# A fused convolution and feed-forward kernel: order and size of the first weight loads, and three matmul units ahead of the first sums of half group 1

## Chip, cores, metric

One core of one Trainium2 chip. The metric is the device time of one execution in microseconds; the "span" of a profile is the time from the first to the last instruction, and lies some 1.7 us below the time of the same execution. Lower is better. Before: 693.21 us (median of 3 runs, 693.14 to 693.33).

## The reference, cut to what matters

```python
w = softmax(weight)                        # 8 heads x 7 taps
x_pad = zeros of 6 rows ahead of x         # x: 8 x 4096 x 192
conv[b, s, h, g] = sum_k w[h, k] * x_pad[b, s + k, h, g]
h = conv.reshape(32768, 192) @ w_in        # 192 x 2048
out = maximum(0.01 * h, h) @ w_out         # 2048 x 192
```

## The kernel before

Everything is kept transposed: channels in the partitions, two batch rows side by side (64 + 64 partitions), three chunks of 64 channels. The first blocks of 512 positions are worked in half groups of 256, so that work can start before much has been loaded. A *unit* of the first matmul makes two of the sixteen 128-wide slices of the hidden layer for one half group: 12 matmuls into one `ph` buffer, which ScalarE evicts through the leaky ReLU into `g`. There are two `ph` buffers. The *sums* are the second matmul, in steps of 32 matmuls.

```python
    pieces = (0, NFC // 4, NFC // 2, NFC)             # NFC = 16; w_in in three tiles: 1/4, 1/4, 1/2
    ...
    def w_in_of(f, ps, c):
        n = max(n for n in range(3) if pieces[n] <= f)
        a = (f // RUN * RUN - pieces[n]) * 128 + f % RUN
        return w_in[n][ps, c, a : a - f % RUN + RUN * 128 : RUN]

    load_w_in(0, 0)                                   # all of these on GpSimd's queue, in this order
    ident = const_pool.tile([128, 128], BF16)
    make_identity(nc, ident)
    load_w_in(0, 1)
    for e in range(2):
        load_w_in(1, e)
    load_first(1)                                     # half 1's x (x_rows)
    for e in range(2):
        load_w_in(2, e)
    load_first(2)                                     # half 2's x
    ...                                               # then w_out, half 3's x, block 2
```

```python
    warm(9)                                           # dummy matmuls, 128x256
    warm(1, 128)
    ...
    select(wps_hm, slice(0, 2))                       # six small matmuls: the taps by channel
    warm(1, 128)
    select(wps_l, 2)                                  # six more
    warm(6)
    ...
    transpose_first(0)                                # half 0's x, on TensorE
    warm(3)
    ...                                               # half group 0's convolution, partly on TensorE (56 matmuls)

        for j in range(steps):
            for u in range(2 * j, 2 * j + 2):
                mm1(grp, u)                           # one unit
                if i == 0 and u == 1:
                    transpose_first(1)                # needs half 1's x
                    evac_first(1, nc.vector.tensor_copy, nc.vector.tensor_copy)
                    ...                               # half group 1's convolution: a chunk on TensorE, two on VectorE
                if i == 0 and u == 3:
                    for job in pe_ahead:
                        job()                         # 28 matmuls
                    evac_y(act_scale)
                if i == 0 and u == 6:
                    transpose_first(2)
            ...
            for _ in range(quota[j]):                 # 0 in half group 0, then 16: one step of sums
                mm2_slot(slot)
                slot += 1
```

Of the kernel before, what the change touches and what calls it, by code (L numbers as in the profile page):

```python
# [14 lines left out]
def kernel(  # L15
# [25 lines left out]
    NFC = F // 128  # L41
# [73 lines left out]
    def load_first(q):  # L115
        rows = x[0:2, q * HT : (q + 1) * HT, :].rearrange("e (s p) d -> p e s d", s=HS)
        if q == 0:
            x_nat[q] = stage_pool.tile([128, 2, HS, D], FP32, name="x_nat")
            for e in range(2):
                nc.sync.dma_start(out=x_nat[q][:, e], in_=rows[:, e])  # L120
        elif q in x_rows:
            for e in range(2):
                nc.gpsimd.dma_start(out=x_rows[q][:, e], in_=rows[:, e])  # L123
        else:
            for c in range(NCH):
                for e in range(2):
                    nc.gpsimd.dma_start(  # L127
                        out=x_half[q][:, c, :, e, :],
                        in_=rows[:, e, :, c * CH : (c + 1) * CH],
                    )  # L130
# [9 lines left out]
    def transpose_first(q):  # L140
        ts = [
            psum_o.tile([128, HS, NCH, CH], BF16, name=f"ptr{i}", tag="po") for i in range(2)
        ]
        for s in range(HS):
            for c in range(NCH):
                for i in range(2):
                    ps = slice(i * CH, (i + 1) * CH)
                    if q in x_half:
                        nc.tensor.transpose(  # L149
                            out=ts[i][:, s, c, :],  # L150
                            in_=x_half[q][ps, c, s, :, :].rearrange("p e k -> p (e k)"),
                            identity=ident[ps, ps],
                        )
                        continue
                    for e in range(2):
                        nc.tensor.transpose(  # L156
                            out=ts[i][e * CH : (e + 1) * CH, s, c, :],
                            in_=x_rows[q][ps, e, s, c * CH : (c + 1) * CH],
                            identity=ident[ps, ps],
                        )  # L160
        ptr[q] = ts

    def evac_first(q, *copies):
        dst = xt[0][:, :, HALO + q * HT : HALO + (q + 1) * HT].rearrange(
            "p c (s i k) -> p i s c k", s=HS, i=2
        )
        for i, t in enumerate(ptr.pop(q)):
            copies[i](out=dst[:, i], in_=t)  # L168
# [4 lines left out]
    def conv_jobs(grp, chunks=range(NCH)):  # L173
        blk, t0, T = grp
        rp, st = divmod(blk, NB)
        if blk not in yt:
            yt[blk] = yt_pool.tile([128, NCH, ST], BF16, name="yt")
        y = yt[blk]
        jobs = []
        for c in chunks:  # L180
            for k in range(K):
                a = BASE + k + st * ST + t0
                src = xt[rp][:, c, a : a + T]
                dst = y[:, c, t0 : t0 + T]
                if k == 0:
                    jobs.append(
                        lambda s=src, d=dst, c=c: nc.vector.tensor_scalar_mul(  # L187
                            d, s, wk[:, c, 0:1]
                        )
                    )  # L190
                else:
                    jobs.append(
                        lambda s=src, d=dst, c=c, k=k: nc.vector.scalar_tensor_tensor(  # L193
                            out=d, in0=s, scalar=wk[:, c, k : k + 1], in1=d,
                            op0=mybir.AluOpType.mult, op1=mybir.AluOpType.add,
                        )
                    )
        return jobs
# [39 lines left out]
        )  # L238


    pieces = (0, NFC // 4, NFC // 2, NFC)
    w_in = [
        const_pool.tile([128, NCH, (b - a) * 128], BF16, name=f"w_in{a}")
        for a, b in zip(pieces[:-1], pieces[1:])
# [2 lines left out]
    def load_w_in(n, e):  # L247
        fs = slice(pieces[n] * 128, pieces[n + 1] * 128)
        nc.gpsimd.dma_start(  # L249
            out=w_in[n][e * CH : (e + 1) * CH],  # L250
            in_=moe_w_in[:, fs].rearrange("(c p) f -> p c f", p=CH),
        )

    def w_in_of(f, ps, c):
        n = max(n for n in range(3) if pieces[n] <= f)
        a = (f // RUN * RUN - pieces[n]) * 128 + f % RUN
        return w_in[n][ps, c, a : a - f % RUN + RUN * 128 : RUN]

# [1 line left out]
    ident = const_pool.tile([128, 128], BF16)  # L260
    make_identity(nc, ident)
    load_w_in(0, 1)
    for e in range(2):
        load_w_in(1, e)
    load_first(1)
    for e in range(2):
        load_w_in(2, e)
    load_first(2)


# [122 lines left out]
    def mm1(grp, u):  # L393
        blk, t0, T = grp
        y = yt[blk]
        nf = ST // T
        ph = psum_h.tile([128, 2, ST], FP32, name="ph", tag="ph")
        for i in range(nf):
            f = nf * u + i
            for c in range(NCH):  # L400
                for e in range(2):
                    ps = slice(e * CH, (e + 1) * CH)
                    nc.tensor.matmul(  # L403
                        out=ph[:, e, i * T : (i + 1) * T],
                        lhsT=w_in_of(f, ps, c),
                        rhs=y[ps, c, t0 : t0 + T],
                        start=(c == 0),
                        stop=(c == NCH - 1),
                    )
        act = nc.scalar.activation(  # L410
            out=g[blk][:, nf * u : nf * (u + 1), :, t0 : t0 + T],
            in_=ph.rearrange("p e (i t) -> p i e t", i=nf),
            func=mybir.ActivationFunctionType.Prelu, alpha=0.01,
        )
        return act
# [83 lines left out]
    for i, grp in enumerate(groups):  # L499
        blk, t0, T = grp  # L500
        steps = T // 64
        if t0 == 0:
            g[blk] = g_pool.tile([128, NFC, 2, ST], BF16, name="g", tag="g")
        quota = plan.get(i, [(avail - slot) // steps] * steps)

        if i == 0:
            ahead = []
        else:
            ahead = conv_jobs(groups[i + 1]) if i + 1 < len(groups) else []
        per = -(-len(ahead) // steps)  # L510
        for j in range(steps):
            for u in range(2 * j, 2 * j + 2):
                mm1(grp, u)
                if i == 0 and u == 1:
                    transpose_first(1)
                    evac_first(1, nc.vector.tensor_copy, nc.vector.tensor_copy)
                    pe_ahead, evac_y = pe_conv_jobs(groups[1], 0)
                    ahead = conv_jobs(groups[1], range(1, NCH))
                    per = len(ahead)
                if i == 0 and u == 3:  # L520

                    for job in pe_ahead:
                        job()
# [3 lines that stand above are left out]
            if i == 1 and j == 3:  # L527
                transpose_first(3)
            jobs = ahead[per * j : per * (j + 1)]
            if T == ST:  # L530


                jobs = ahead[len(ahead) * j // steps : len(ahead) * (j + 1) // steps]
                for job in jobs:
                    job()
                jobs = []
            for _ in range(quota[j]):
                mm2_slot(slot)
                slot += 1
            if i == 0 and j == 3:  # L540
                evac_first(2, nc.vector.tensor_copy, nc.vector.tensor_copy)
            if i == 2 and j == 1:
                transpose_x(2)
            for job in jobs:
                job()
            if i == 1 and j == 3:
                evac_first(3, nc.vector.tensor_copy, nc.vector.tensor_copy)

            last_half = t0 + T == ST
            if j == steps // 4 and last_half:  # L550
                load_x(blk + 3)
            if j == steps // 2 and last_half and blk > 0:
                transpose_x(blk + 2)
        avail += 2 * T // 128 * NFC
# [36 lines left out]
```

## Time and profile before

| what (us from the start) | before |
|---|---|
| time, span of the profiled run | 693.21; 690.9 |
| TensorE busy | 684.0 of 690.9 |
| second part of the first unit starts | 10.15 |
| first sums start | 22.48 |
| between the two | 12.33 |
| w_in's first tile, second tile landed | 8.1, 11.8 |
| half 1's x landed | 13.0 |
| third w_in tile, half 2's x, w_out landed | 16.8, 17.8, 21.6 |

Landings are read from the trace's landing records, and a landing here is the last of a transfer's 16 records: for the two parts of half 1's x these came at 12.50 and 13.03, and TensorE's waits for them ended at 12.55 and 13.07.

The timeline of TensorE stands in the prediction. Columns: start, length, engine, line, operation, operands, shapes, count, and in brackets the idle time before it and what ended it.

```profile
6.33 3.26 PE L212 MATMUL acc<-xt,diag 64*64 64x256 bf16 x56 [0.17 <-ACT xt L168]
```

The 56 matmuls take 3.26 us, 58 ns each: TensorE at full clock, by the clock record of this trace (1.0 from 5.38 us on).

### The profile page before, as it was taken

To read this page: it belongs to the slowest core of one execution; us is meant where nothing else is said; L and a number is where in the kernel's file an instruction comes from. 1 tells how busy PE (TensorE), PEld (TensorE's weight loads), DVE (VectorE), ACT (ScalarE), POOL (GpSimd) and SP (SyncE) were. 2 spreads that over 40 slices of the span, in tenths; PEclk is the share of its full clock that TensorE was granted. 3 is DMA by queue.
4 is the path that set the end of the run, shared out by engine and by line. 5 is a ranking of instruction groups with operands and counts; after the bars stand their busy time and mean duration, and the time that the engine had idled before them with its cause. 6 is when DMAs were issued, how large, how long until landed. Compare 5 with 4: busy or idle time off the path is not lost.

```text
span 690.9 us, 26980 instructions
## 1 busy us (share of the span) xinstructions
PE 684.0 (99%) x12188; PEld 599.2 (87%) x12188; DVE 550.1 (80%) x1051; ACT 527.0 (76%) x609; POOL 147.1 (21%) x206
## 2 busy tenths in 40 slices
PE   8999999999999999999999999999999999999998
PEld 6999999999988888888888888888888888888887
DVE  6999999999986787878787878877878878787812
ACT  6888888888898777777777777777777777777771
POOL 7822220222222202222102222102222112000000
PEclk9999999999999999999999999999999999999999
DMA  9976454556649445566445565445664455322112
GB/s 153 117 92 94 76 79 82 68 75 83 82 71 94 72 81 74 67 93 82 67 84 68 75 83 87 74 74 76 77 82 74 81 73 70 67 60 59 47 42 65
DMA packets 184163, 53.85 MB, mean 78 GB/s; under 512 B 149104, under 2 KB 183664, under 8 KB 184048
## 3 DMA queue, kind: packets, MB, share of 16 engines
q0 software_dynamic: 99536, 14.76, 30.2%
q1 hardware_dynamic: 84512, 37.38, 22.8%
q8 instruction: 95, 1.56, 1.0%
q14 instruction: 20, 0.16, 0.1%
HBM read 29.88 MB, written 25.17 MB: 80 GB/s over the span
## 4 chain that ended last, share of the span: by engine, by line
PE 96%; ACT 1%; DMA 1%; POOL 1%; issue 0%; DVE 0%; POOLq 0%
PE po L429 49%; PE ph L403 47%; ACT g L410 1%; DMA w_in<-in_moe_w_in_dram 1%; POOL w_in L249 0%; POOL x_rows L123 0%; POOL sel L234 0%; DVE o_sb L476 0%; PE ptr L156 0%; POOL ident masks.py:199 0%; POOL sel L232 0%; POOL ident masks.py:197 0%; PE ptr L149 0%; POOLq masks.py:199 0%; POOLq L575 0%
## 5 line engine op out<-in xcount | busy, mean ns | idle before, releaser
L410 ACT ACTIVATE g<-ph 128x1024 bf16<-128x1024 f32 x512 | 496.2, 1021 | 143.2 <-PE ph L403 142.7
L193 DVE SCALAR_TENSOR_TENSOR yt<-xt,wk,yt 128x512 bf16<-128x512 bf16 (+1 forms) x720 | 458.3, 637 | 21.1
L429 PE MATMUL po<-w_out,g 64*128 64x192 bf16 (+1 forms) x8064 | 387.7, 243 | 0.0
L403 PE MATMUL ph<-yt,w_in 64*128 64x512 bf16 (+1 forms) x3936 | 384.7, 329 | 1.3 <-ACT g L410 0.7
L429 PEld LDWEIGHTS <-g 64*128 64x128 bf16 (+1 forms) x8064 | 360.5, 94 | 28.8 <-issue 0.2
L403 PEld LDWEIGHTS <-w_in 64*128 64x128 bf16 x3936 | 245.0, 111 | 54.6 <-issue 3.5
L78 POOL DMA_DIRECT2D x_bf<-in_x_dram x180 | 133.7, 777 | 424.6 <-DMA xt<-x_bf 422.0
L476 DVE COPY o_sb<-po 128x192 f32<-128x192 f32 x184 | 65.6, 357 | 109.1 <-PE po L429 100.4
L187 DVE TENSOR_SCALAR yt<-xt,wk 128x512 bf16<-128x512 bf16 (+1 forms) x120 | 40.6, 338 | 1.7 <-DMA xt<-x_bf 1.5
L476 ACT COPY o_sb<-po 128x192 f32<-128x192 f32 x72 | 23.0, 319 | 3.9 <-PE po L429 0.2
L284 PE MATMUL warm<-zero 128*128 128x256 bf16 (+1 forms) x20 | 4.5, 384 | 1.1 <-DVE junk L229 1.1
L212 PE MATMUL acc<-xt,diag 64*64 64x256 bf16 x84 | 5.0, 269 | 0.2 <-ACT xt L168 0.2
L168 DVE COPY xt<-ptr 128x384 bf16<-128x384 bf16 x7 | 2.2, 351 | 3.6 <-PE ptr L156 3.6
L212 PEld LDWEIGHTS <-diag 64*64 64x64 bf16 x84 | 4.5, 106 | 0.6 <-DVE xt L168 0.3
L127 POOL DMA_DIRECT2D x_half<-in_x_dram x6 | 4.3, 717 | 3.0 <-DMA w_in<-in_moe_w_in_dram 3.0
L284 PEld LDWEIGHTS <-zero 128*128 128x128 bf16 x20 | 2.4, 132 | 2.0 <-DVE junk L229 1.1
L249 POOL DMA_DIRECT2D w_in<-in_moe_w_in_dram x6 | 3.9, 656 | 0.0
L345 ACT ACTIVATE diag<-ident,whm 128x64 bf16<-128x64 bf16 x14 | 3.5, 335 | 0.0
L123 POOL DMA_DIRECT2D x_rows<-in_x_dram x4 | 2.9, 736 | 0.0
L156 PE MATMUL ptr<-ident,x_rows 64*64 64x64 bf16 x48 | 1.0, 196 | 1.3 <-DMA x_rows<-in_x_dram 1.3
L156 PEld LDWEIGHTS <-x_rows 64*64 64x64 bf16 x48 | 0.6, 108 | 1.9 <-DMA x_rows<-in_x_dram 1.7
L371 ACT ACTIVATE yt<-acc,rsum 128x256 bf16<-128x256 f32 x3 | 1.4, 467 | 1.0 <-PE acc L212 1.0
(37 smaller groups left out, 12.6 us busy)
## 6 DMA issues: line engine op xcount, KB each, us to landing
out_dram<-o_sb SPq DMA_DIRECT2D x117, 192.0 KB, 2.1
x_bf<-in_x_dram POOLq DMA_DIRECT2D x180, 64.0 KB, 3.3
out_dram<-o_sb SPq DMA_DIRECT2D x22, 96.0 KB, 1.6
xt<-x_bf SPq DMA_TRANSPOSE x90, 2.5
w_in<-in_moe_w_in_dram POOLq DMA_DIRECT2D x4, 192.0 KB, 5.6
w_in<-in_moe_w_in_dram POOLq DMA_DIRECT2D x2, 384.0 KB, 9.1
w_out<-in_moe_w_out_dram POOLq DMA_DIRECT2D x1, 768.0 KB, 11.2
x_nat<-in_x_dram SPq DMA_DIRECT2D x2, 192.0 KB, 2.6
```

Of the source, the lines that this page charges most:

```text
L78: nc.gpsimd.dma_start(out=t[:, c, :, e, :], in_=src[2 * rp + e, :, :, c * CH : (c + 1) * CH],)
L127: nc.gpsimd.dma_start(out=x_half[q][:, c, :, e, :], in_=rows[:, e, :, c * CH : (c + 1) * CH],)
L187: lambda s=src, d=dst, c=c: nc.vector.tensor_scalar_mul(d, s, wk[:, c, 0:1])
L193: lambda s=src, d=dst, c=c, k=k: nc.vector.scalar_tensor_tensor(out=d, in0=s, scalar=wk[:, c, k : k + 1], in1=d, op0=mybir.AluOpType.mult, ...
L212: lambda k=k, p=p, a=a, e=e, ps=ps: nc.tensor.matmul(out=acc[ps, :T], lhsT=diag[c][ps, p, k, :], rhs=xt[0][ps, c, a : a + T], start=(k == ...
L249: nc.gpsimd.dma_start(out=w_in[n][e * CH : (e + 1) * CH], in_=moe_w_in[:, fs].rearrange("(c p) f -> p c f", p=CH),)
L284: nc.tensor.matmul(out=wa[:, 0, 0:cols], lhsT=zero[:, 0:128], rhs=zero[:, 0:cols], start=True, stop=True,)
L345: nc.scalar.activation(out=diag[c][:, p, k, :], in_=ident2, func=mybir.ActivationFunctionType.Copy, scale=whm[:, c, p, k : k + 1],)
L403: nc.tensor.matmul(out=ph[:, e, i * T : (i + 1) * T], lhsT=w_in_of(f, ps, c), rhs=y[ps, c, t0 : t0 + T], start=(c == 0), stop=(c == NCH - 1),)
L410: act = nc.scalar.activation(out=g[blk][:, nf * u : nf * (u + 1), :, t0 : t0 + T], in_=ph.rearrange("p e (i t) -> p i e t", i=nf), func=my ...
L429: return nc.tensor.matmul(out=po[m], lhsT=g[b][ps, fc, e, s * 128 : (s + 1) * 128], rhs=w_out[ps, fc, :], start=start, stop=stop,)
L476: ins = copy(out=o_sb[:, n % 2, :], in_=po.pop(n))
```

## The change

Its intent: TensorE waited for half 1's x, which stood in the queue behind w_in's second tile, and for the second half of w_in, which came as one large tile. So the x goes up behind the first quarter, and the half becomes two quarters. With TensorE earlier, w_out might be late for the first sums; a third unit goes ahead of them.

```diff
-    pieces = (0, NFC // 4, NFC // 2, NFC)
+    pieces = range(0, NFC + 1, NFC // 4)
...
-        n = max(n for n in range(3) if pieces[n] <= f)
+        n = f // pieces[1]
...
     load_w_in(0, 1)
-    for e in range(2):
-        load_w_in(1, e)
     load_first(1)
-    for e in range(2):
-        load_w_in(2, e)
+    for n in range(1, len(w_in)):
+        for e in range(2):
+            load_w_in(n, e)
     load_first(2)
...
         for j in range(steps):
-            for u in range(2 * j, 2 * j + 2):
+            units = range(2 * j, 2 * j + 2)
+            if i == 1 and j < 2:
+                units = (range(3), range(3, 4))[j]
+            for u in units:
                 mm1(grp, u)
```

## The prediction

> **What bounds the kernel now.** I read the page first (engine totals, chain, waits), then the chain of waits over the whole span, then the timeline engine by engine over the first 32 us, because the change touches nothing later.
>
> ```profile
> PE 684.0 (99%) x12188; PEld 599.2 (87%) x12188; DVE 550.1 (80%) x1051; ACT 527.0 (76%) x609; POOL 147.1 (21%) x206
> PE 96%; ACT 1%; DMA 1%; POOL 1%; issue 0%; DVE 0%; POOLq 0%
> ```
>
> TensorE is the bound, and the change removes no matmul. It can only win back idle or stretched TensorE time: 690.9 - 684.0 = 6.9 us idle in all, part of it at the very end. So 2% (13.9 us) is out of reach, and the question is about tenths. Here is TensorE's timeline (start, length, what; in brackets the idle time before and what ended it):
>
> ```profile
> 10.15 1.40 PE L403 MATMUL ph<-yt,w_in 64*128 64x256 bf16 x22 [0.33 <-ACT yt L371]
> 12.55 0.21 PE L156 MATMUL ptr<-ident,x_rows 64*64 64x64 bf16 x1 [1.00 <-DMA x_rows<-in_x_dram]
> 13.07 0.38 PE L156 MATMUL ptr<-ident,x_rows 64*64 64x64 bf16 x23 [0.31 <-DMA x_rows<-in_x_dram]
> 13.38 1.50 PE L403 MATMUL ph<-yt,w_in 64*128 64x256 bf16 x24
> 14.81 1.72 PE L212 MATMUL acc<-xt,diag 64*64 64x256 bf16 x28
> 16.47 1.85 PE L403 MATMUL ph<-yt,w_in 64*128 64x256 bf16 x24
> 18.78 0.85 PE L403 MATMUL ph<-yt,w_in 64*128 64x256 bf16 x12 [0.46 <-ACT g L410]
> 19.55 0.38 PE L156 MATMUL ptr<-ident,x_rows 64*64 64x64 bf16 x24
> 19.87 1.74 PE L403 MATMUL ph<-yt,w_in 64*128 64x256 bf16 x24
> 21.83 0.85 PE L403 MATMUL ph<-yt,w_in 64*128 64x256 bf16 x12 [0.22 <-ACT g L410]
> 22.48 1.52 PE L429 MATMUL po<-w_out,g 64*128 64x192 bf16 x32
> 23.80 1.51 PE L403 MATMUL ph<-yt,w_in 64*128 64x256 bf16 x24
> ```
>
> A unit of the first matmul is 12 matmuls. Undisturbed, 24 of them take 1.31 us from start to start (23.80 to the next sums at 25.11), so a unit costs 0.655 us. From the end of units 0 and 1 (11.55) to the first sums (22.5 here, 22.68 in the chain, which counts from the last matmul's end) TensorE does units 2 to 7 and units 0 and 1 of half group 1 (8 x 0.655 = 5.24), the 28 matmuls of the convolution (1.66) and two sets of transposes (0.31 each): 7.5 us of work in 11.1 us. **Some 3.6 us are lost here**: 1.31 to half 1's x, 0.24 and some stretch to the third w_in tile, 0.68 to ScalarE, and more within the 1.85 and 1.74 (half group 1's first unit also needs VectorE's last convolution chunk, done at 20.9).
>
> ScalarE and VectorE in the same stretch, and GpSimd's issues, whose start shows which landing let the next transfer go:
>
> ```profile
> 14.27 1.94 ACT L410 ACTIVATE g<-ph 128x1024 bf16<-128x1024 f32 x2 [1.41 <-PE ph L403]
> 16.58 0.47 ACT L371 ACTIVATE yt<-acc,rsum 128x256 bf16<-128x256 f32 x1 [0.37 <-PE acc L212]
> 17.70 6.04 ACT L410 ACTIVATE g<-ph 128x1024 bf16<-128x1024 f32 x6 [0.65 <-PE ph L403]
> 13.49 0.62 DVE L168 COPY xt<-ptr 128x384 bf16<-128x384 bf16 x2 [3.55 <-PE ptr L156]
> 20.84 0.61 DVE L168 COPY xt<-ptr 128x384 bf16<-128x384 bf16 x2
> 10.41 0.76 POOL L272 DMA_DIRECT2D w_out<-in_moe_w_out_dram  x1 [1.23 <-DMA w_in<-in_moe_w_in_dram]
> 21.90 2.23 POOL L78 DMA_DIRECT2D x_bf<-in_x_dram  x3 [2.64 <-DMA w_out<-in_moe_w_out_dram]
> ```
>
> ScalarE evicts six units in a row from 17.70 at 6.04 / 6 = 1.0 us each: with no sums between, units cost ScalarE more than TensorE, and the two ph buffers make TensorE follow it. VectorE sat 3.55 us waiting for half 1's transposes. The view of transfers, asked around each issue, gives landings (last of the 16 engines): w_in's first tile 6.6 and 8.1, its second 10.1 and 11.8, half 1's x 12.5 and 13.03, its third 14.95 and 16.77, half 2's x 17.3 and 17.9, w_out 21.6. GpSimd's waits fit eight transfers in flight: the eleventh (w_out) left when the third landed, the nineteenth when the eleventh (w_out) did.
>
> The same view over two stretches shows that packet size matters. From 4.5 to 8 us almost all packets are w_in's of 1,024 B; from 13.5 to 16.5 they are 2,048 B (third w_in tile) and 384 B (x):
>
> ```profile
> DMA packets 498, 0.47 MB, mean 135 GB/s; under 512 B 37, under 2 KB 498, under 8 KB 498
> DMA packets 723, 0.60 MB, mean 201 GB/s; under 512 B 493, under 2 KB 573, under 8 KB 723
> ```
>
> [...] the second half of the second w_in tile has most engines in by 10.5 and the last at 11.8. [...] in this trace's packet records the typical packet takes 51 ns at 384 B, 98 at 1,024 and 173 at 2,048, so two quarters cost 2 x 98 = 196 where a half tile cost 173. [...]
>
> **The change, part by part.**
>
> *Half 1's x ahead of w_in's second tile.* The queue up to 13.03 holds the same bytes. The x (192 KB) took 1.25 us on the typical engine (10.2 to 11.45); put behind the first tile's 8.1 it is in by some 9.7, before TensorE asks at 11.55. The waits of 1.00 and 0.31 go. But units 2 and 3, next in order, need w_in's second tile, now last of the same bytes: in at about 13.0. So TensorE does the transposes at 11.55 and waits again; units 2 and 3 start at 12.95 instead of 13.38. **This gains 0.4 us on TensorE, not 1.3.** VectorE gains more: its copies start at 11.95 instead of 13.49, so half 1's last chunk (7.4 us on) is done at 19.35 instead of 20.9.
>
> *Quarters three and four.* The first 384 KB of the second half of w_in arrive in a tile of their own, in by some 15.4 instead of 16.77; units 4 and 5 need only them, and TensorE asks for them at 16.05 (12.95 + 1.43 + 1.66). The wait at 16.8 goes. The last quarter: 48 packets per engine in place of 24. At 98 ns with the overlap seen (24 packets of 173 took 3.75 us, 0.9 of the sum) 48 take 4.25 us, 0.5 more; at the pace of the second tile, where some packets stalled (24 in 2.7 us), 5.4, 1.6 more. So it is in at 17.2 to 18.4, half 2's x at 18.4 to 19.2, and **w_out at 22.1 to 23.2 instead of 21.6**. Two more issues on GpSimd (0.63 each) lie in its 1.23 of waiting.
>
> *TensorE from there.* Unit 4 at 16.05, its eviction (behind the 0.47 of the scaling) 16.9 to 17.9, unit 5's to 18.85. Unit 6 needs that first buffer and the last quarter: 17.95 to 18.4. Transposes at some 19.1 to 19.5 with half 2's x; unit 7 ends near 20.0 to 20.4; half group 1's unit 0 needs unit 6's eviction (19.9 to 20.3), unit 1 unit 7's (20.95 to 21.35), and the added third unit needs unit 0's (21.95 to 22.3). It ends at 22.65 to 23.0.
>
> *Three units first.* The first sums then start at the later of that and w_out's landing: 22.65 to 23.2. That point has one unit, 0.655, more behind it than the 22.68 of before, so it equals 22.0 to 22.55: **0.15 to 0.7 us gained, 0.45 in the middle.** Unit 3 alone (0.655) then covers the 0.19 us pass of ScalarE between the rounds of sums. Afterwards the steps of 2.63 us are as before; VectorE, close to the bound (half group 2's convolution ended at 31.66, its unit 0 began at 31.87), comes 1.0 to 1.5 us earlier, so more than TensorE, and doesn't stop it.
>
> **The rivals.** (1) *w_out becomes the wait.* For: it landed at 21.6, only 0.9 before it was wanted, and quarters can delay it by 0.5 to 1.6. Against: the third unit pushes the need back to 22.65 or later. At 23.5 or later the gain is gone or becomes a loss of 0.2: 693.2 to 693.4. (2) *All idle time goes.* For: ScalarE waited 1.41 for units 2 and 3, and everything behind them could move up if w_in's second tile landed sooner than its bytes say. Then w_out at 21.65 with a unit more ahead is the floor: 22.68 - 21.0 = 1.7 at most, 691.5. (3) *ScalarE sets the pace.* Six evictions, one scaling and the first of half group 1, at about 1.0 each, follow the start of units 2 and 3; whatever the transfers do, the gain is then that start's 0.4 plus a little: 692.7.
>
> **Range and chances.** Three is what my working amounts to, with (1) trimming it. 693.2 - 0.45 = 692.75. Low: two thirds of (2), 691.9. High: 693.4, a loss of 0.2 with w_out late. The profiled run took 692.65 against 693.14 to 693.33 timed, so 0.3 is noise between runs. Over 2% either way would need 13.9 us; neither a whole early stretch of waits (3.6) nor a doubled w_out delay gets there.
>
> **What would show it.** Right: no wait on x_rows at 12.55 and VectorE's copies near 12.0; a wait of about 1 us on w_in before units 2 and 3, near 13.0; no wait on w_in at 16.8; TensorE on ScalarE's pace from 17.9; w_out at 22.1 to 23.2; 36 matmuls of L403 in half group 1 before the first L429, at 22.6 to 23.2; the pages after 32 us alike but for the shift. Wrong: units 2 and 3 at 12 or earlier (second tile sooner), L429 waiting on w_out's transfer past 23.3, or a new wait on yt.

Cut from it are figures that no trace of this case shows, and a rule drawn from them for reordered transfers. No term of its sum is cut: it came to 693.2 - 0.45 = 692.75 us. One step, w_in's second tile in at about 13.0 although it now comes last, rests on 13.03 as the landing of the same bytes in the old order; that the order wouldn't change it was the author's estimate, not shown.

## The result

693.29 us (median of 4 runs, 692.94 to 693.92) against 693.27 (median of 4, 693.14 to 693.46). The ratio is 1.0001, 95% interval 0.9984 to 1.0018; ratios are the mean time of one kernel's fast runs over the mean of the other's of the same rounds, so not quite the ratio of the medians. The time hasn't moved, and the changed kernel's runs lie further apart.

The profile of the changed kernel, TensorE's timeline:

```profile
6.57 4.90 PE L212 MATMUL acc<-xt,diag 64*64 64x256 bf16 x56
12.04 1.39 PE L402 MATMUL ph<-yt,w_in 64*128 64x256 bf16 x22 [0.34 <-ACT yt L370]
13.36 0.38 PE L156 MATMUL ptr<-ident,x_rows 64*64 64x64 bf16 x24
13.89 1.77 PE L402 MATMUL ph<-yt,w_in 64*128 64x256 bf16 x24
15.58 1.72 PE L212 MATMUL acc<-xt,diag 64*64 64x256 bf16 x28
17.24 1.50 PE L402 MATMUL ph<-yt,w_in 64*128 64x256 bf16 x24
19.20 0.85 PE L402 MATMUL ph<-yt,w_in 64*128 64x256 bf16 x12 [0.46 <-ACT g L409]
22.26 1.76 PE L402 MATMUL ph<-yt,w_in 64*128 64x256 bf16 x24 [0.25 <-ACT g L409]
23.82 1.52 PE L428 MATMUL po<-w_out,g 64*128 64x192 bf16 x32
```

No wait for a transfer is left: the one on x_rows is gone and the stretched 1.85 us of units 4 and 5 is 1.50. From the second part of the first unit (12.04) to the first sums (23.82) it takes 11.78 us, with one more unit inside; less its 0.655 that is **11.13 us where it was 12.33: 1.2 us won.** But the stretch begins at 12.04 instead of 10.15: **1.9 us lost ahead of anything the change touches.** The top line shows where: the same 56 matmuls of the convolution took 4.90 us instead of 3.26. The group of that line on the two pages, first before, then after (mean ns of one matmul after the comma):

```profile
L212 PE MATMUL acc<-xt,diag 64*64 64x256 bf16 x84 | 5.0, 269 | 0.2 <-ACT xt L168 0.2
```

```profile
L212 PE MATMUL acc<-xt,diag 64*64 64x256 bf16 x84 | 6.6, 325 | 0.0
```

The instructions are the same, and so is all that TensorE runs ahead of them; no line of the timeline shows it waiting between the start of the warm-up and the end of the convolution. What differs is the clock. The trace's clock record has full clock from 5.38 us on in the profile of before, and only from 9.99 us on in this one. (The page's row of granted clock shows 9 in all slices of both, and asking for 4 to 7 us gives 1.00: the record begins with the rise, and what lies ahead of it is counted as full. A mean of 325 for 269 ns is the visible sign, and so are the starts: in this trace two of the 56 matmuls take some 213 ns from start to start up to 9.98 us and some 109 from there on; in that of before all take some 109.)

So theory A: by chance, this run's clock rose later, at 9.99 us for 5.38; the change is worth about 1 us when the clock rises early. Rival B: the change is worth nothing, and its stretch was short only because the transfers had time to land while TensorE was slow. Rival C: the change itself delays the clock.

### The profile page after: what moved, and what is told of

The parts are those of the page before. It is cut to its first block, busy times and chain, and to the rows that moved or that the text cites. A ratio compares the mean times of both kernels' runs of the same rounds, so it can differ in the third digit from the quotient of the medians.

```text
span 691.7 us, 26982 instructions
## 1 busy us (share of the span) xinstructions
PE 686.0 (99%) x12188; PEld 601.1 (87%) x12188; DVE 551.0 (80%) x1051; ACT 527.2 (76%) x609; POOL 148.5 (21%) x208
## 3 DMA queue, kind: packets, MB, share of 16 engines
q8 instruction: 95, 1.56, 1.0%
## 4 chain that ended last, share of the span: by engine, by line
PE 97%; ACT 2%; issue 0%; DVE 0%
PE po L428 48%; PE ph L402 47%; ACT g L409 2%; PE acc L212 1%; PE warm L283 1%; PE ptr L149 0%; ACT yt L370 0%; DVE o_sb L475 0%; PE ptr L156 0%; PE wps L319 0%; PE wps_l L319 0%; DVE zero L227 0%; DVE junk L229 0%
## 5 line engine op out<-in xcount | busy, mean ns | idle before, releaser
L212 PE MATMUL acc<-xt,diag 64*64 64x256 bf16 x84 | 6.6, 325 | 0.0
(37 smaller groups left out, 11.8 us busy)
```

The costliest lines, as they stand in the source:

```text
L212: lambda k=k, p=p, a=a, e=e, ps=ps: nc.tensor.matmul(out=acc[ps, :T], lhsT=diag[c][ps, p, k, :], rhs=xt[0][ps, c, a : a + T], start=(k == ...
```

## The experiments

"Stretch" is always from the second part of the first unit to the first sums, less 0.655 us where a third unit is inside.

### The changed kernel again

No edit.

> The changed kernel once more, unaltered, for a second profile and five more pairs of times. Theory A (the TensorE clock's rise falls by chance at about 5.4 or about 9.8 us after the start, and the change itself is worth about 1 us from the first matmul's start to the first sums): times spread over about 1.5 us, mean within 0.5 us of the kernel before; if this profile has the clock up by 6 us, its span is 689.6 to 690.3, if only near 9 to 10 us, 691.3 to 692. Rival B (the change is worth nothing, its shorter stretch in the first profile came only from transfers having time to land while TensorE was slow): with an early clock the span is 690.7 to 691.1, as before. Rival C (the change itself delays the clock): the clock is late again in this profile.

Measured: 693.29 us (median of 6, 691.69 to 694.97), the kernel before 693.13 (median of 11, 692.34 to 694.38); ratio 1.0002, 0.9989 to 1.0016. This profile's clock rose at 4.72 us, and its span is 690.0:

```profile
6.60 3.26 PE L212 MATMUL acc<-xt,diag 64*64 64x256 bf16 x56 [0.54 <-ACT xt L168]
10.42 1.39 PE L402 MATMUL ph<-yt,w_in 64*128 64x256 bf16 x22 [0.33 <-ACT yt L370]
12.27 1.76 PE L402 MATMUL ph<-yt,w_in 64*128 64x256 bf16 x24
22.20 1.52 PE L428 MATMUL po<-w_out,g 64*128 64x192 bf16 x32
```

The stretch is 11.13 us, to the hundredth that of the first profile (22.20 - 10.42 - 0.655), and the span is 0.9 below that of before. So rivals B and C fall for an early clock: with TensorE early, the change saves 0.9 us, by one profile of each kernel. The spread came out wider than expected, 3.3 us, not 1.5.

w_out landed at 22.11 us here, a tenth ahead of the first sums: the third unit did cover it.

### Both kernels held back until the clock is surely up

```diff
+            hold = const_pool.tile([128, 1024], BF16, name="hold")
+            for _ in range(10):
+                nc.gpsimd.memset(hold, 0.0)
+            nc.gpsimd.memset(x_nat[q][:, :, 0, 0:1], 0.0)
...
+    warm(45)
     warm(9)
```

> The kernel before, with everything held back: ten memsets on GpSimd ahead of its first work and of the first x transfer, and 45 more warm-up matmuls, so that the clock is up before the convolution [...]. Only a yardstick for the other held kernels. About 8 to 11 us longer than the kernel before[...].

> The changed kernel held back in the same way. Theory A: 0.6 to 1.3 us faster than h_before (the working in the prediction said 0.15 to 0.7). Rival B: within 0.2 us of h_before. In the trace: no wait on x_rows; a wait on w_in of 0.5 to 1 us before units 2 and 3; w_out landed before the first sums ask for it.

A third, with only the order of the loads changed (the hunk that moves `load_first(1)`; w_in stays in three tiles):

> Held back, and of the change only half 1's x ahead of w_in's second tile (thirds stay as they were, no third unit ahead). My working: units 2 and 3 start about 0.4 to 0.7 us earlier and the third w_in tile is waited for as before, so 0.0 to 0.5 us faster than h_before; rival: it carries the whole gain of h_after.

**This experiment failed in what it was built for.** Medians 702.41, 702.23 and 702.89 us (4 runs each), spreads of 1.6, 0.9 and 0.8. The extra warm-up ended before GpSimd's memsets did, TensorE sat idle for 2.1 to 2.8 us, and the clock fell back: in the kernel held back before, idle from 9.11 to 11.95, it was full from 4.97 to 11.80 us, half to 18.62. The convolution was slow in all three (4.53, 5.23 and 5.29 us). That makes them a test of the other case, TensorE late, and a weak one: the clock rose at 18.62, 19.96 and 20.11 us, so the three did not start the first unit at the same time, and only the stretch can be compared. The medians lie within the spread of each other (the changed kernel 0.18 below before), as rival B expected. Before, then changed:

```profile
15.96 4.53 PE L216 MATMUL acc<-xt,diag 64*64 64x256 bf16 x56
21.05 1.39 PE L408 MATMUL ph<-yt,w_in 64*128 64x256 bf16 x22 [0.33 <-ACT yt L376]
31.93 1.52 PE L434 MATMUL po<-w_out,g 64*128 64x192 bf16 x32
```

```profile
21.66 1.39 PE L407 MATMUL ph<-yt,w_in 64*128 64x256 bf16 x22 [0.33 <-ACT yt L375]
31.88 1.76 PE L407 MATMUL ph<-yt,w_in 64*128 64x256 bf16 x24 [0.25 <-ACT g L414]
33.45 1.51 PE L433 MATMUL po<-w_out,g 64*128 64x192 bf16 x32
```

With TensorE late, the stretch of *before* is 10.88 us and it waits for no transfer (half 1's x landed at 22.39, asked for at 22.38); with the new order alone 10.87; with the whole change 11.13 (33.45 - 21.66 - 0.655). So here the change *costs* 0.25 us, and it is the third unit: units 1 and 2 of half group 1 take 1.57 us (31.88 to 33.45), not 1.31, since the third must wait until ScalarE has evicted the first (its eviction ended at 32.74, the third unit began at 32.79). Rival B is right for a late clock.

Together: the changed kernel took 11.13 us in all three of its profiles, with TensorE early or late, and the kernel before 12.33 with it early and 10.88 with it late. Before swallows a late clock in its waits; the changed kernel passes it on. The estimate for an unaltered kernel before with a late clock, from these: 12.04 + 10.88 + 668.4 (from the first sums to the end; 668.4 to 668.7 in all the profiles, with 0.655 added where the third unit came first) = 691.3 us of span, against 691.7 measured for the changed one; with an early clock 690.9 against 690.0. A gain of 0.9 in some runs and a loss of 0.4 in others: that is how a mean near nothing can come about. It is an estimate: no profile of the unaltered kernel before with a late clock was taken, and what share of the runs came late is not known (the granted clock listed for a run counts the time ahead of the rise as full: 1.000 for the profile with the rise at 9.99). Nor does it explain everything: with 1.7 us added to a span, it puts the changed kernel at 691.7 or 693.4 us, and single runs went up to 694.97.

### A steadier warm-up

What could put the rise off? In the late profile TensorE had, ahead of it, both small selects (3.27 to 3.5 and 3.74 to 4.0 us) and half 0's transposes (5.4 to 5.9). The two early profiles have the same instructions, so these alone don't make the difference; that they leave the rise to chance was the guess, which no trace had shown. It is what was tried: in both kernels, one select in place of two, and half 0's transposes as ordinary matmuls against the identity:

```diff
-    warm(9)
+    warm(10)
     warm(1, 128)
...
-    select(wps_hm, slice(0, 2))
-    warm(1, 128)
-    select(wps_l, 2)
-    warm(6)
+    select(wps_all, slice(0, 3))
+    warm(7)
...
+                    if q == 0:
+                        nc.tensor.matmul(
+                            out=ts[i][:, s, c, :],      # fp32 here
+                            lhsT=x_half[q][ps, c, s, :, :].rearrange("p e k -> p (e k)"),
+                            rhs=ident[ps, ps], start=True, stop=True,
+                        )
```

> The kernel before with a steadier warm-up: the three parts of the weights selected in one go of six small matmuls in place of two of six, half 0's transposes as ordinary matmuls into fp32, two more warm-up matmuls. Theory A [...]: the clock is up by 8 us in every profile of the steadier kernels; the time is within 0.5 us of the kernel before, since before has its waits for transfers whether TensorE comes early or not (first sums 12.3 us after the first unit when early, 10.9 when late). Rival: the late clock comes back in some of these profiles.

> The changed kernel with the steadier warm-up. Theory A: clock up early, from the second part of the first unit (10.2 to 10.5 us) to the first sums 11.8 us (11.13 and the third unit's 0.655), 0.6 to 1.2 us faster than r_before in the profile's span and some 0.8 in the mean time, spread narrower than the 3.3 us of the changed kernel. Rival B [...]: within 0.2 us of r_before.

(Theory A is here the guess above.)

And the changed kernel without the third unit (`for u in range(2 * j, 2 * j + 2)` as before), and of the change the new order alone:

> The changed kernel with the steadier warm-up and without the third unit ahead. If w_out lands at 21.4 to 22.1 as in the two profiles of the changed kernel, the first sums can't start before that, where TensorE is done with two units at about 21.3: so a wait of 0.1 to 0.8 us on w_out, and 0.1 to 0.6 us slower than r_after. If the third unit is only a cost (0.25 us by the held kernels): up to 0.25 faster than r_after.

> The kernel before with the steadier warm-up and of the change only half 1's x ahead of w_in's second tile. My working: no wait on x_rows, units 2 and 3 at 12.3 to 12.9, then a wait on the third w_in tile (landing 16.1 to 16.8) of 0.3 to 1 us; 0.2 to 0.6 us faster than r_before. If the order alone made the gain, as fast as r_after.

Three of them once more, with one that splits w_out:

> The kernel before with the steadier warm-up, again: its last profile waited 2.12 us on half 1's x, where the unaltered kernel waited 1.31, and its mean was 1.1 us over the unaltered kernel's. If that was a slow transfer engine by chance, this profile's wait is 1.0 to 1.5 us and the mean 0 to 0.5 us over the kernel before; if the steadier warm-up harms the transfers, as last time. Either way 0.5 us or more above the changed kernel with the same warm-up.

> The changed kernel with the steadier warm-up again, for a second profile and five more times. Theory A: clock up by 8 us, 11.8 us from the second part of the first unit to the first sums, 668.2 to 668.4 us from there to the end; mean time 692.0 to 692.8.

> The changed kernel with the steadier warm-up without the third unit, again: the five times before this were 0.5 us below those with the third unit, where the profiles say 0.2 to 0.3 above. If the profile is right, the mean is now 0 to 0.5 us above the one with the third unit; if the times are, 0.3 to 0.7 below.

The kernel before without a steadier warm-up ran beside them: 693.21 us in the mean of all its 33 runs (692.34 to 694.53).

| steadier warm-up, and | clock up at (us) | stretch (us) | span (us) | mean time, lowest to highest (us) |
|---|---|---|---|---|
| before | 6.20; not recorded | 13.49; 12.07 | 692.5; 691.9 | 693.50 of 10 runs, 692.01 to 694.75 |
| new order alone | 6.39 | 11.86 | 690.7 | 692.38 of 5, 692.30 to 692.51 |
| order and quarters | 6.03; 4.25 | 11.48; 11.80 | 690.2; 690.4 | 691.94 of 10, 691.33 to 692.48 |
| the whole change | 6.44; 5.23 | 11.17; 11.22 | 690.0; 689.8 | 692.23 of 10, 691.49 to 693.93 |

**The clock.** Of these seven profiles and that of the next section, seven have a clock record, and in all of them it was up by 7.3 us; in the eighth, whose record is missing, the convolution took the same 3.26 us as with an early clock. The edit is the only difference; but one late clock in three unaltered profiles leaves some chance that eight early ones were luck, so it is likely, not proved, that the edit did it. Its parts weren't tried alone. The times point the same way: the steadier warm-up takes the changed kernel from 693.24 (mean of its 10 runs) to 692.23, 1.0 us, 95% interval 0.2 to 1.8, and gains nothing in the kernel before (693.21 and 693.50). (The two sets ran on different chips; the kernel before, which ran beside both, had means of 693.1 to 693.3 on each.) So most of what the change had lost lay, by these times, in the start of TensorE.

**The gain.** The whole change against before, with the same warm-up: 692.23 against 693.50, 1.27 us faster, 95% interval 0.5 to 2.1 (each half by itself: 1.56 and 0.97). That is 0.2% and shows only with the clock in hand. Part of it is that before came out slow: its x landed at 14.1 and 13.7 instead of 13.0. Its first profile, then the same points of the whole change:

```profile
10.37 1.40 PE L411 MATMUL ph<-yt,w_in 64*128 64x256 bf16 x22 [0.33 <-ACT yt L379]
13.39 0.21 PE L166 MATMUL ptr<-ident,x_rows 64*64 64x64 bf16 x1 [1.62 <-DMA x_rows<-in_x_dram]
14.10 0.38 PE L166 MATMUL ptr<-ident,x_rows 64*64 64x64 bf16 x23 [0.50 <-DMA x_rows<-in_x_dram]
18.20 1.50 PE L411 MATMUL ph<-yt,w_in 64*128 64x256 bf16 x23 [0.41 <-DMA w_in<-in_moe_w_in_dram]
23.86 1.52 PE L437 MATMUL po<-w_out,g 64*128 64x192 bf16 x32
```

```profile
10.37 1.40 PE L410 MATMUL ph<-yt,w_in 64*128 64x256 bf16 x22 [0.33 <-ACT yt L378]
22.20 1.52 PE L436 MATMUL po<-w_out,g 64*128 64x192 bf16 x32
```

The typical transfer engine had that x in at 11.56, as in the unaltered profile (11.48); the last came 2.5 us behind it instead of 1.5. The second profile had 2.2 us. I had put it down to chance or to the warm-up; the second run, with a wait of 1.06 on x and a mean of 692.79, came out as chance would have it, but its transfers were still a little late, so this stays half open.

Three of the ten runs of before with the steadier warm-up (694.26, 694.49, 694.75) have a granted clock of 0.998: by estimate 2 to 3.5 us at half clock somewhere in the span, if it fell to half as in the kernel held back before (0.995, with 6.82 us at half). Two of the runs of before without it have the same (694.38, 694.53); these five are the slowest of all runs in the order of before, and none of the 40 runs with x ahead (the held kernels aside) has it. Without the three, before with the steadier warm-up is at 693.07, level with the kernel before, and the gain of the whole change is 0.84 (interval 0.1 to 1.6). Why their clock was lower isn't shown: no profile of such a run was kept.

**The parts.** The order alone takes the stretch to 11.86, with two waits left, for the second and the third w_in tile:

```profile
12.84 1.50 PE L410 MATMUL ph<-yt,w_in 64*128 64x256 bf16 x23 [0.35 <-DMA w_in<-in_moe_w_in_dram]
16.57 1.50 PE L410 MATMUL ph<-yt,w_in 64*128 64x256 bf16 x23 [0.35 <-DMA w_in<-in_moe_w_in_dram]
```

The quarters end the second of them, and then w_out is the wait that takes its place:

```profile
21.84 1.50 PE L436 MATMUL po<-w_out,g 64*128 64x192 bf16 x32 [0.41 <-DMA w_out<-in_moe_w_out_dram]
```

The third unit covers that one: 11.17 against 11.48. In the second pair it was 11.22 against 11.80, but there w_in's second tile cost 0.82 us in the kernel without the third unit, and w_out nothing. In the times the third unit shows no gain (692.23 with, 691.94 without, an interval from 0.3 faster to 0.9 slower): the spans favour it by 0.2 to 0.6 and the means don't settle it. Nor do they settle the quarters: in the same rounds the order alone took 692.38, the whole change 692.64, order and quarters 692.12. Of the expectations, the 0.1 to 0.6 that leaving out the third unit should have cost did not come (0.52 faster in the first set, 0.06 in the second), and the order alone came out 1.8 us below before of the same rounds, not 0.2 to 0.6, because that before was slow. So the times show that x ahead is worth having; what the quarters and the third unit add stands on single profiles.

### w_out in two tiles

```diff
-    w_out = const_pool.tile([128, NFC, D], BF16)
-    nc.gpsimd.dma_start(...)
+    w_outs = [const_pool.tile([128, NFC // 2, D], BF16, name=f"w_out{h}") for h in range(2)]
+    for h in range(2):
+        nc.gpsimd.dma_start(...)                      # half of the rows each
```

on the changed kernel with the steadier warm-up and without the third unit.

> The changed kernel with the steadier warm-up, without the third unit, and with w_out in two tiles loaded one after the other, so that the first sums need only its first half. If w_out's last bytes alone held the first sums back where two units stand ahead (0.41 us in the run without the third unit), the first half is in by about 20.5 us, the sums start at 21.2 to 21.5 us with no wait, 10.8 to 11.0 us after the second part of the first unit, and the span is 689.3 to 689.8; 0.3 to 0.6 us faster than the changed kernel with the steadier warm-up. If the extra transfer slows the queue, or another load is the last to come, no faster.

Measured: 691.99 us (median of 5, mean 692.15), span 690.6. A miss. The first half of w_out was in at 20.17, and the sums at 22.17 waited for nothing; but in this run w_in's second tile came at 13.37:

```profile
13.42 1.50 PE L413 MATMUL ph<-yt,w_in 64*128 64x256 bf16 x23 [0.59 <-DMA w_in<-in_moe_w_in_dram]
```

Without those 0.59 us the stretch would be 10.86 instead of 11.45, what the expectation said. (The clock rose at 7.26 in this run, and the convolution took 3.57 us instead of 3.26.) The wait that the split removes isn't always the last one: which load is late differs from run to run.

The version that beats both kernels is thus not this one. The changed kernel with the steadier warm-up, with or without the third unit, is 1.0 and 1.3 us faster than the kernel before (692.23 and 691.94 against 693.21 of 33; intervals 0.4 to 1.5 and 1.0 to 1.6), some 0.15 to 0.2%. (The 33 are from the four sets of rounds in which these kernels and the others ran.)

## Why the prediction was right

The time lay where it said, within 2% and between 691.9 and 693.4. By its steps:

- **TensorE is the bound, and tenths are at stake.** Right. From the first sums to the end all profiles take 668.4 to 668.7 us, the third unit counted, so what follows is only shifted.
- **Half 1's x ahead: the waits of 1.00 and 0.31 go.** Right, in every profile. VectorE's copies at 12.0: 12.17 in the second profile; not in the first (13.79), as TensorE was late.
- **Units 2 and 3 wait for w_in's second tile until 12.95, so 0.4 us are won and not 1.3.** Right in kind, wrong in size. That tile landed at 12.37 and 12.28 in the two profiles of the changed kernel, and units 2 and 3 began at 12.27 with the early clock, with no wait on w_in instead of one of about 1 us. (ScalarE's eviction of unit 0 had ended at 12.22, so an earlier tile would not have moved unit 2 there.) In the steadier kernels it landed between 11.8 and 13.4, and TensorE waited 0, 0.35, 0.59 and 0.82 us. "Now last of the same bytes: in at about 13.0" took one run's slowest engine, 1.5 us behind the typical one, for a constant: over GpSimd's loads of the first 24 us the last engine came 0.5 to 1.7 us behind in the profile of before and 0.9 to 1.2 in the first of the changed kernel.
- **Quarters three and four: no wait at 16.8.** Right.
- **w_out at 22.1 to 23.2 because of the smaller packets.** Wrong: 21.39 and 22.11, the second at the lower edge only because its last engine was 1.8 us behind. On the typical engine it came at 20.32 and 20.30 instead of 20.05, so 0.3 us later where the step had 0.5 to 1.6. The stalled packets of the first microseconds, which made the upper end, hardly came back for the last quarters (packets of 1,024 B over 150 ns, in the first profile: 11% of those begun from 4 to 8 us, 3% after 10.5).
- **The third unit ends at 22.65 to 23.0, and the gain is 0.15 to 0.7.** With the clock early the first sums began at 22.20, and the span fell by 0.9: more than that. With the clock late the third unit costs 0.25.
- **0.3 us is noise between runs.** This failed. Its own figures, 692.65 against 693.14 to 693.33, are 0.5 to 0.7 apart; the kernel before ranged over 2.2 us in 33 runs, the changed one over 3.3 in 10. The term that is missing from the sum is TensorE's own start: 10.42 or 12.04, by when the clock rose. The prediction took the 10.15 of one profile for given; it forecast a gain of 0.45 and the mean gain was none (693.24 of 10 runs against 693.21). That a late clock takes back what an early one lets through is what the profiles and the steadier warm-up support; that it is the whole of it isn't shown.
- **Rival (3), ScalarE's pace, is what the working amounts to.** Borne out: with no transfer in the way TensorE waits some 0.46 and 0.25 us for evictions in every profile, and the third unit runs on that pace. That is why the stretch comes out at the same 11.13 us with the clock early or late.
- **Two small sums don't come out:** two thirds of the 1.7 in rival (2) give 692.1 at the low end, not 691.9, and half 2's x delayed by up to 1.6 would be in at 19.4, not 19.2. Nothing hangs on either.

So the time lay in the range, and that is partly luck: the stretch gained more than forecast with the clock early, and the clock, which the working doesn't have, took it back. The range reached up to 693.4 for a late w_out, which did not come.

## What to carry to other kernels

Waits in a start-up stretch run side by side with other delays: taking them away is worth what is left once the other delay is counted, here TensorE's clock, which rose at 4.72 us in one profile of the same kernel and at 9.99 in the other. Before comparing two profiles over a microsecond, check that the same instructions at the start took the same time in both; where they did not, look at the clock record and take another profile. Here a warm-up with fewer small matmuls, and with half 0's transposes made ordinary matmuls, brought the gain into the mean times (692.23 against 693.50 us).
